# Attention and feed-forward in one kernel: score products in pairs of heads on the two halves of TensorE's rows, and weight scales from column sums

## The chip, the core and the metric

The program runs on one core of a Trainium2 chip. The metric is the device time of one launch in microseconds (us), lower is better. A core has the engines TensorE (PE; PEld is its weight load), VectorE (DVE), ScalarE (ACT), GpSimd (POOL) and SyncE (SP, which here only issues DMAs). Each takes its instructions in program order, and they wait for each other by semaphores. Products of TensorE go to eight banks of an accumulator memory, PSUM.

## The reference, cut

```python
# q, k, v: (8 batches, 8 heads, 576 positions, 64); w_in (512, 2048); w_out (2048, 512), all float32
scores = np.matmul(q, k.transpose(0, 1, 3, 2)) / 8
rel = pos[:, None] - pos[None, :]
mask_plain = (rel >= 0) & (rel < 32)                        # heads 0 to 3
mask_dil = (rel >= 0) & (rel < 128) & (rel % 4 == 0)        # heads 4 to 7
attn = softmax(where(mask, scores, -1e9))
x = (attn @ v), heads side by side: (4608, 512)
h = x @ w_in
g = h * np.tanh(np.log1p(np.exp(h)))                        # mish
out = g @ w_out                                             # (4608, 512)
```

## The kernel before

The 4608 rows are worked on as 16 units `u` of 288 positions (half a batch each). All large products are made of float16 parts: a float32 number is scaled by a power of two and split into a high and a low float16 half, and three of the four products of halves are summed in PSUM. So a unit's first feed-forward product (`ff1`, one step `ff<u>.<fc>` for each of 16 column groups) is 12 TensorE products with 288 moving columns, and so is each step of its second (`ff2`, steps `fo<u>.<e>.<j>`, 4 output groups by 4 chunks of the sum). That makes 512 steps in all, 6144 products.

Attention of a unit: `loads` and `loads_v` fetch q, k and v; `prep` finds scales; `scores` (`sc`) multiplies; `exps` (`ex`), `transpose_p` (`tp`), `values` (`va`), `transpose_x` (`tx`) follow. A head has few key blocks because of its mask: 3 blocks of 96 queries by 96 or 128 keys (heads 0 to 3) or 4 blocks of 72 queries by 72 or 104 keys (heads 4 to 7). Units 0 to 3 are *direct*: `scores` starts a PSUM bank with the mask (L628) and adds float32 products of one head (L632). A head has 64 dimensions, so an even head lies in partitions 0 to 63 and an odd one in 64 to 127, and such a product uses 64 of TensorE's 128 rows. Units 4 to 15 are *split*: `prep` makes float16 halves `q2` and `k2` (L540 to L559), and 12 DMAs of SP (L555, L556, L566) then copy them so that the high and the low half of one head stand under each other in 128 partitions (`qs`, `ks`). With that a block takes two products with all 128 rows (L638).

The weights come as 64-bit floats, 16 chunks of 1 MB in the order of steps `wl<k>.<g>.<p>` (`k` 0 for w_in, 1 for w_out; `g` a group, `p` one of its two chunks). For each chunk `w_max` takes a maximum on VectorE (L311, tile `am`) and a scaled copy on ScalarE (L366); for each group `w_scale` brings the maximum over partitions by a transposition and a product (L319, L328) and computes the scale on VectorE; `w_words` (L406, L407, L409) builds float32 words and `w_split` the two halves, in ways that the table `WAYS` picks. Everything of `early`, the raw weights included, has to be done with before `open_late` can hand that memory to the split units.

`ORDER` is a list written out by hand: a name stands once for each stage of its step (a stage ends at a `yield`), and each engine gets its instructions in that order. `kw<n>` (`keep_warm`, L920) puts `n` products of zeros on TensorE as filler. Four PSUM banks (tag `a`) serve scores, values and transpositions, four others (tag `f`) the feed-forward and the filler. `BIASED`, `ON_POOL`, `ON_PE` and `ON_ACT` say which engine does a stage of some steps.

Of the kernel before, what the change touches and what calls it, by code (L numbers as in the profile page):

```python
# [32 lines left out]
TINY_HI = 0.05859375  # L33
# [16 lines left out]
va2.1 tp2.2 wp0.2.1 tp2.6 va2.2 ff0.12 va2.2 ff0.13 wp0.2.0 ff0.14 ff0.15 va2.2 wm0.0.0 ff0.8 gt0.1 gt0.3 ff0.10 va2.1  # L50
ww0.0.0 ff0.8 wp0.0.1 tx2.0 tp2.3 va2.6 ff0.11 tx2.0 va2.6 tp2.3 ff0.10 tp2.4 tx2.0 ff0.9 ff0.11 va2.6 tp2.4 gt0.3
wp0.0.0 va2.3 tp2.5 wp0.0.1 va2.3 ff0.9 tp2.5 gt0.2 va2.3 wl1.1.0 wp0.0.0 tx2.1 va2.4 tx2.1 va2.5 gt0.2 va2.4 wl1.0.0
tx2.1 va2.5 tp2.7 tx2.1 ff0.0 wl1.0.1 tp2.7 va2.4 wl1.1.1 va2.5 va2.7 ff0.0 ff0.1 lv1 va2.7 va2.7 tx2.2 ff0.1 tx2.3
ff0.3 tx2.2 ld1 wm1.1.0 tx2.3 tx2.2 ff0.2 tx2.2 tx2.3 wm1.1.0 ff2.0 ff0.3 ww1.1.0 ff0.2 ff2.1 ff2.0 gt0.0 ff2.2 ff2.1
wm1.0.0 gt0.0 ff2.4 ff2.2 wm1.0.0 ff2.5 ff2.4 wm1.0.1 ff2.6 ff2.5 wm1.0.1 ff2.7 ff2.6 ff2.3 ff2.7 gt2.1 wm1.1.1 ws1.0
ff2.3 gt0.0 ws1.0 ws1.1 wm1.1.1 ws1.0 ws1.1 ws1.0 ws1.1 gt2.0 ws1.1 gt2.1 ff2.8 pr1 gt2.1 wp1.1.0 ff2.10 ff2.11 gt2.0
ff2.8 ff2.10 ff2.9 ww1.1.1 ff2.11 sc1.3 ff2.9 gt2.2 ww1.0.1 sc1.2 sc1.1 ff2.12 sc1.3 wp1.1.0 sc1.2 ex1.3 ff2.15 gt2.2
ff2.14 ex1.2 ff2.12 wp1.1.1 tp1.2 sc1.0 sc1.1 wp1.1.1 tp1.2 sc1.4 ff2.15 sc1.0 ff2.14 sc1.7 ex1.1 sc1.4 sc1.5 sc1.7
tp1.3 wp1.1.1 ff2.13 sc1.5 tp1.3 wp1.1.1 ex1.4 pr1 fo2.1.0 ex1.5 ex1.7 pr1 wp1.0.1 pr1 fo2.1.1 ex1.0 pr1 wp1.0.1
ff2.13 sc1.6 fs1 va1.2 sc1.6 ld3 va1.3 gt2.3 tp1.0 fo2.1.2 ww1.0.0 lv3 va1.3 tp1.0 va1.2 ex1.6 tp1.1 fo0.1.0 va1.2  # L60
gt2.3 wl1.2.0 va1.3 va1.0 tp1.1 wp1.0.0 fo0.1.1 wp1.0.1 gt2.3 va1.0 tp1.6 va1.0 va1.1 tp1.6 fo0.1.2 va1.1 va1.1
wp1.0.0 tp1.5 sc3.4 tp1.5 sc3.2 sc3.4 wp1.0.1 wp1.0.0 sc3.6 sc3.2 ex3.4 sc3.3 sc3.6 wp1.0.0 fo2.1.3 ex3.2 sc3.3 ex3.6
pr3 tx1.0 ex3.3 tx1.1 fo2.0.0 tx1.0 fo2.1.3 va1.6 tx1.1 tx1.0 tp1.4 va1.6 wm1.2.0 fo2.0.1 tx1.0 tp1.4 va1.6 wm1.2.0
va1.4 tx1.1 fo2.0.2 va1.4 tx1.1 ww1.2.0 va1.5 sc3.7 va1.5 va1.4 tp1.7 fo2.0.3 sc3.7 tp1.7 va1.5 ex3.7 sc3.0 fo2.0.3
sc3.1 sc3.0 va1.7 sc3.1 ld4 ex3.0 sc3.5 fo0.1.3 ex3.1 sc3.5 wl1.2.1 va1.7 tx1.2 va1.7 ex3.5 tp3.4 fo2.0.3 fo0.0.0
tx1.2 fo2.1.3 wl1.3.1 tp3.4 tx1.2 tx1.3 tp3.0 wl1.3.0 tx1.3 fo0.0.1 tp3.0 tx1.3 pr3 tx1.3 fo0.0.2 pr3 pr4 lv4 ff1.0
pr4 pr4 pr3 fo0.0.3 ff1.0 pr3 va3.0 wm1.2.1 va3.4 va3.0 va3.4 tp3.1 tp3.2 tp3.1 va3.0 wm1.2.1 va3.4 va3.1 fo0.1.3
ws1.2 va3.1 tp3.3 tp3.2 va3.1 tp3.3 fo0.1.3 ff1.4 fo0.0.3 ws1.2 ww1.2.1 fo0.0.3 ff1.7 ff1.4 ff1.1 ff1.7 wm1.3.1 ws1.2
ff1.2 ff1.1 ws1.2 wm1.3.1 wp1.2.0 ff1.6 ff1.2 ww1.3.1 ff1.3 ff1.6 ff1.5 wp1.2.1 ff1.3 wm1.3.0 wp1.2.0 ff1.12 ff1.5
gt1.1 pr4 ff1.13 wp1.2.1 ff1.12 wp1.2.0 ff1.14 ff1.13 wp1.2.0 wp1.2.1 pr4 ws1.3 tx3.0 pr4 ff1.15 ff1.14 ws1.3 tx3.0  # L70
wp1.2.1 wm1.3.0 pr4 va3.2 pr4 ws1.3 fo2.2.0 ff1.15 va3.2 gt1.3 ws1.3 va3.3 fo2.2.1 va3.2 va3.3 wp1.3.1 tp3.6 va3.3
fo2.2.2 wp1.3.1 tp3.6 tx3.0 fs3 tp3.5 fs4 tx3.1 tp3.5 fo2.2.3 wp1.3.1 ww1.3.0 tx3.1 va3.5 fo0.2.0 fo2.2.3 va3.5
fo2.2.3 fo0.2.1 va3.5 wp1.3.1 wp1.3.0 tx3.1 tx3.2 fo0.2.2 tx3.2 wp1.3.0 va3.6 fo0.2.3 tx3.2 va3.6 mr ol pr4 va3.6
tp3.7 fo0.2.3 fo0.3.0 fo0.2.3 fo2.3.0 tp3.7 pr4 va3.7 fo2.3.1 va3.7 pr4 fo2.3.2 fo2.3.3 va3.7 pr4 tx3.3 fo2.3.3
fo0.3.1 tx3.3 fo2.3.3 tx3.3 fo0.3.2 gt1.0 fo0.3.3 gt1.0 pr4 fo0.3.3 ff1.8 fo0.3.3 gt1.1 ff1.11 pr4 ff1.8 gt1.3 ff1.10
ff1.11 gt1.1 fo1.3.0 ff1.10 ff1.9 gt1.3 ld5 fo1.3.1 ff1.9 gt1.2 ff3.0 gt1.2 pr4 sc4.2 sc4.1 sc4.6 sc4.2 sc4.5 ff3.1
ff3.0 pr4 fo1.3.2 ff3.1 sc4.0 fo1.3.3 sc4.1 lv5 fo1.3.3 pr5 sc4.4 ff3.2 fo1.3.3 sc4.6 ff3.3 ff3.2 pr5 sc4.7 sc4.5
ff3.3 ff3.4 pr5 sc4.3 ff3.4 ff3.5 sc4.0 ff3.6 ff3.5 pr5 ff3.7 ff3.6 ff3.8 sc4.4 ff3.7 pr5 sc4.7 ff3.8 ff3.9 pr5 ff3.10
ff3.9 sc4.3 pr5 ff3.10 ff3.11 pr5 ex4.1 fo1.2.0 fs5 pr5 fo1.2.1 fo1.2.2 tp4.1 fo1.0.0 pr5 tp4.1 tp4.1 fo1.0.1 ex4.7
pr5 ex4.6 ex4.3 fo1.0.2 ex4.2 ex4.0 fo1.0.3 tp4.2 pr5 tp4.0 tp4.2 ex4.5 tp4.0 fo1.2.3 ex4.4 fo1.0.3 ff3.11 tp4.0  # L80
fo1.1.0 fo1.2.3 tp4.2 tp4.5 tp4.3 fo1.1.1 tp4.5 gt3.0 tp4.3 fo1.0.3 pr5 tp4.5 va4.0 tp4.7 va4.1 fo1.1.2 gt3.1 tp4.3
gt3.0 va4.0 va4.2 va4.1 tp4.4 pr5 fo1.1.3 va4.2 tp4.6 gt3.1 ff3.12 gt3.2 va4.2 va4.0 va4.3 ff3.12 ff3.13 gt3.2 va4.3
ld6 ff3.14 va4.3 ff3.13 va4.1 tp4.7 tx4.0 tp4.4 ff3.14 tp4.7 tp4.6 tx4.1 tx4.0 fo1.1.3 sc5.1 pr5 tp4.4 sc5.2 sc5.0
tx4.1 sc5.4 sc5.1 ff3.15 tx4.0 tx4.1 fo3.0.0 pr5 ff3.15 gt3.3 tp4.6 sc5.7 fo3.0.1 fo1.2.3 gt3.3 lv6 fo3.0.2 pr6
fo3.1.0 fo1.1.3 sc5.2 fo3.1.1 pr6 va4.6 sc5.0 fo3.1.2 va4.6 pr6 fo3.0.3 va4.6 pr6 va4.7 fo3.0.3 fo3.1.3 va4.7 fo3.0.3
# [131 lines left out]
def attn_mish_ffn_kernel(  # L217
# [91 lines left out]
    def amax(o, i, axes=None):  # L309
        axes = axes or {2: AX.X, 3: AX.XY, 4: AX.XYZ}[len(i.shape)]  # L310
        nc.vector.tensor_reduce(o, i, axis=axes, op=ALU.max, apply_absolute_value=True)  # L311

    ones = const.tile([8, 1], F32, name="ones")
    nc.vector.memset(ones, 1.0)

    def over_partitions(m, n):
# [660 lines left out]
```

## Time and profile before

| | us |
|---|---|
| three runs | 960.72, 966.01, 969.75 |
| median of them | 966.01 |
| the profiled execution's own time | 960.96 |
| its span, first to last instruction | 959.1 |
| mean granted TensorE clock in it | 0.973 |

The page of the profile gives busy time by engine, the busy share in 40 slices of the span, the chain of work that ended last and groups of instructions by line. For TensorE busy time is no measure of use: its products are pipelined, so a product is on record for about 290 ns while the next one starts after 122 ns. What counts there is the time from start to start, which the timeline shows.

### The profile page before, as it was taken

What the parts mean: (1) busy time and instruction counts of PE and PEld (TensorE: products, weight loads), DVE (VectorE), ACT (ScalarE), POOL (GpSimd) and SP (SyncE); (2) the same over time, 40 slices, a digit from 0 to 9 for tenths busy, and PEclk for the clock granted to TensorE, in tenths of its full rate; (3) what the DMA queues carried; (4) which work ended last, traced back from release to release, by engine and by line L of the source; (5) the groups of instructions that cost most, each with busy time, mean ns of one, the idle gap of its engine ahead of it and who ended that gap; (6) DMA issues with size and microseconds to landing.
All of it is one profiled execution on the core that took longest, in us unless ns stands there. A gap on an engine that the chain in (4) does not pass through costs nothing.

```text
span 959.1 us, 21690 instructions
## 1 busy us (share of the span) xinstructions
PE 926.6 (97%) x8761; PEld 753.1 (79%) x8761; DVE 670.2 (70%) x1389; ACT 563.4 (59%) x1074; POOL 63.7 (7%) x117
## 2 busy tenths in 40 slices
PE   7998899999999899999989999999999999999998
PEld 6876678787877678888878887888888888887776
DVE  5789698695668777796959695887868696841020
ACT  2668676554373665738566665566665757555151
POOL 1000324033200000000000000000001000000000
PEclk7789999999999999999999999999999999999999
DMA  7523505601538392737385756748382826150000
GB/s 254 167 88 102 166 1 160 211 1 48 152 73 188 77 181 67 175 82 164 85 163 85 154 117 120 144 97 173 73 173 64 181 71 151 37 101 4 26 1 26
DMA packets 169620, 105.57 MB, mean 110 GB/s; under 512 B 126800, under 2 KB 156208, under 8 KB 169520
## 3 DMA queue, kind: packets, MB, share of 16 engines
q1 hardware_dynamic: 169520, 104.18, 46.0%
q8 instruction: 69, 1.13, 0.5%
q14 instruction: 31, 0.25, 0.1%
HBM read 49.02 MB, written 9.44 MB: 61 GB/s over the span
## 4 chain that ended last, share of the span: by engine, by line
PE 82%; DVE 8%; DMA 3%; issue 3%; SPq 3%; ACT 2%; POOL 0%; DVEq 0%; POOLq 0%; ACTq 0%
PE po L891 35%; PE ph L840 33%; PE psc L638 3%; PE pav L748 3%; PE psc L632 3%; SPq L566 2%; DMA pT<-p 1%; PE pav L742 1%; PE pz L920 1%; DVE g L881 1%; DVE raw L407 1%; DVE raw L409 1%; PE psc L628 1%; DMA g<-g 1%; DMA ks<-k 1%
## 5 line engine op out<-in xcount | busy, mean ns | idle before, releaser
L840 PE MATMUL ph<-x,w 128*128 128x288 f16 x3072 | 398.2, 289 | 2.5 <-DVE w L426 2.5
L891 PE MATMUL po<-g,w 128*128 128x288 f16 x3072 | 390.0, 287 | 0.0
L840 PEld LDWEIGHTS <-w 128*128 128x128 f16 x3072 | 298.9, 99 | 78.4 <-DVE w L426 2.6
L891 PEld LDWEIGHTS <-w 128*128 128x128 f16 x3072 | 298.4, 98 | 74.3 <-issue 0.2
L845 ACT ACTIVATE hm<-ph,fs 128x288 f32<-128x288 f32 x256 | 125.7, 498 | 137.5 <-PE ph L840 136.9
L881 DVE SCALAR_TENSOR_TENSOR g<-hm,sg,g 128x1152 f16<-128x1152 f32 x59 | 83.3, 1413 | 84.3 <-ACT g L879 84.3
L903 ACT ACTIVATE y<-po,fo 128x288 f32<-128x288 f32 x57 | 41.9, 736 | 134.5 <-PE po L891 115.5
L879 ACT ACTIVATE g<-hm,sg 128x1152 f16<-128x1152 f32 x59 | 74.0, 1254 | 4.6 <-PE po L891 3.6
L765 DVE TENSOR_TENSOR xs<-pav,rec 96x192 f32<-96x192 f32 (+1 forms) x128 | 49.6, 387 | 11.1
L654 DVE TENSOR_TENSOR sb<-sb,nm 96x256 f32<-96x256 f32 (+3 forms) x120 | 54.5, 454 | 4.1
L652 DVE TENSOR_REDUCE nm<-sb 96x2 f32<-96x256 f32 (+3 forms) x120 | 53.7, 448 | 3.3
L712 DVE TENSOR_TENSOR p<-sb,p 72x288 f16<-72x288 f32 (+3 forms) x57 | 28.7, 523 | 38.4 <-ACT p L710 38.4
L674 ACT ACTIVATE sb<-sb,ln_p 72x288 f32<-72x288 f32 (+3 forms) x96 | 51.6, 583 | 0.1
L646 DVE SCALAR_TENSOR_TENSOR sb<-psc,sc,m_r 96x352 f32<-96x352 f32 (+1 forms) x48 | 28.4, 591 | 23.5 <-PE psc L638 23.5
L522 POOL PARTITION_ALL_REDUCE mru<-m x10 | 10.8, 1077 | 495.6 <-DVE m L311 286.9
L638 PE MATMUL psc<-ks,qs 128*96 128x128 f16 (+3 forms) x672 | 41.2, 211 | 1.0 <-DMA ks<-k 1.0
L712 DVE TENSOR_TENSOR g<-sb,g 72x416 f16<-72x416 f32 (+3 forms) x39 | 20.2, 528 | 28.6 <-ACT g L710 28.5
L638 PEld LDWEIGHTS <-qs 128*72 128x72 f16 (+1 forms) x672 | 37.5, 119 | 2.4 <-DMA ks<-k 1.4
L780 ACT CAST g<-xs 96x384 f16<-96x384 f32 (+1 forms) x48 | 26.7, 556 | 16.0 <-DVE xs L765 15.9
L540 ACT ACTIVATE q<-qn,s 128x144 f16<-128x144 f32 (+1 forms) x60 | 30.5, 584 | 4.9 <-DVE s L307 4.8
L763 DVE RECIPROCAL rec<-den 96x3 f32<-96x3 f32 (+1 forms) x128 | 21.2, 165 | 15.4 <-ACT den L759 9.6
L782 DVE TENSOR_TENSOR g<-xs,g 96x384 f16<-96x384 f32 (+1 forms) x48 | 29.5, 614 | 2.5 <-ACT g L780 2.3
(139 smaller groups left out, 966.7 us busy)
## 6 DMA issues: line engine op xcount, KB each, us to landing
qn<-in_qT SPq DMA_DIRECT2D x16, 576.0 KB
out_T<-y SPq DMA_DIRECT2D x64, 144.0 KB
ks<-k SPq DMA_DIRECT2D x48, 184.0 KB
raw<-in_w_in SPq DMA_DIRECT2D x16, 512.0 KB
raw<-in_w_out SPq DMA_DIRECT2D x16, 512.0 KB
qs<-q SPq DMA_DIRECT2D x48, 144.0 KB
ks<-k SPq DMA_DIRECT2D x48, 144.0 KB
vn<-in_v SPq DMA_DIRECT2D x48, 128.0 KB
```

Of the source, the lines that this page charges most:

```text
L638: nc.tensor.matmul(pt[:nq, col:col + nk], d["qs"][:, h, pair, q0:q0 + nq], d["ks"][i][:, h, k0:k0 + nk], start=(i == 0), stop=(i == 1))
L652: nc.vector.tensor_reduce(nm[:nq, j:j + n], x, axis=AX.X, op=ALU.max, negate=True)
L654: nc.vector.tensor_tensor(o, x, nm[:nq, j:j + n].unsqueeze(2).broadcast_to([nq, n, w]), op=ALU.add)
L674: nc.scalar.activation(x, x, AF.Exp, bias=ln_p[:nq])
L712: nc.vector.tensor_tensor(lo, src, hi, op=ALU.subtract)
L765: nc.vector.tensor_tensor(xs[:nq, :nb, (head % 2) * D:(head % 2 + 1) * D], avv[:, :, :D], rc.unsqueeze(2).broadcast_to([nq, nb, D]), op=AL ...
L840: nc.tensor.matmul(ph[:, :HT], w1[j][:, c, wi, k * P:(k + 1) * P], x_of(d, xi, c), start=(n == 0), stop=(n == len(seq) - 1))
L845: nc.scalar.activation(d["m"][j][:, k], ph[:, :HT], AF.Mish, scale=d["fs"][:, j:j + 1])
L879: nc.scalar.activation(g[:, 0], m, AF.Identity, scale=sg)
L881: nc.vector.scalar_tensor_tensor(g[:, 1], m, sg, g[:, 0], ALU.mult, ALU.subtract)
L891: nc.tensor.matmul(po[:, :HT], w2[:, e, j, wi, k * P:(k + 1) * P], d["g"][j][:, gi, k, :], start=(j == 0 and n == 0), stop=(j == NCH - 1 a ...
L903: nc.scalar.activation(o, src, AF.Identity, scale=fo)
```

## The change

Split units: the copies to `qs` and `ks` go. Scores come from `q2` and `k2` where they lie, three products with 64 rows for a block instead of two with 128. `q2` and `k2` get a second buffer.

All units: a new step `sp<u>.<pair>` (`scores_of_pair`) makes the products of an even and an odd head together and lets them take turns, so that one product uses rows 0 to 63 and the next rows 64 to 127; it fills two of the four banks of tag `a`. `sc` keeps the work on VectorE.

Weights: the maximum on VectorE and the way over partitions go. `w_scale` multiplies the scaled copy, read as bfloat16, by ones on TensorE, so that every partition has the column sums in PSUM, and takes their maximum (L374). It is 4 products of 512 columns for a group of w_in and 16 of 128 for one of w_out. `w_words` becomes two stages. The constants of the scales and four ways of `WAYS` change.

`ORDER` is new: weights and units come in another sequence, v of unit 0 is the first load, and the filler grows from 238 to 646 products, all but 7 of them ahead of the first feed-forward product. The filler no longer takes a bank in turn, it writes the last 128 columns of one that the feed-forward uses. The tables change in a few entries.

```diff
     def w_max(k, g, p):
-        if k == 0:
-            amax(am[:, p:p + 1], hi.bitcast(F32))
-        else:
-            amax(am[:, p * WIDE:(p + 1) * WIDE], hi.bitcast(F32), AX.X)
-        yield
         nc.scalar.activation(a, hi.bitcast(F32), AF.Identity, scale=HI)
     def w_scale(k, g):
+        pm = ps.tile([P, 512], F32, tag="a", name="pm", bufs=4)
+        for i in range(NCC):
...
+            if k == 0:
+                nc.tensor.matmul(pm, ones_b.broadcast_to([P, P]), top, start=(i == 0), stop=(i == NCC - 1))
+            else:
+                for q in range(FPC):
+                    nc.tensor.matmul(pm[:, i * P:(i + 1) * P], ones_b.broadcast_to([P, P]), top[:, q * P:(q + 1) * P],
+                                     start=(q == 0), stop=(q == FPC - 1))
+        yield
+        nc.vector.tensor_reduce(m, pm.rearrange("p (a n) -> p a n", a=n), axis=AX.X, op=ALU.max)
...
     def prep(u):
-        for h in range(2):
-            nc.sync.dma_start(qs[0:D, h], qh[hs])
-            nc.sync.dma_start(qs[D:P, h], ql[hs])
...
-                for o in range(2):
-                    nc.sync.dma_start(ks[i][o * D:(o + 1) * D, h, :nkall], src[hs, :nkall])
+    def scores_of_pair(u, pair):
...
+        for h in range(2):
+            pt = d["ps", 2 * pair + h] = ps.tile([P, 512], F32, tag="a", name="psc", bufs=4)
...
+                for i, (qi, ki) in enumerate([(1, 0), (0, 0), (0, 1)]):
+                    products.append((o, d["q2"][hs, qi, pair, q0:q0 + nq], d["k2"][hs, ki, k0:k0 + nk], i == 0, i == 2))
...
+        for both in zip(*heads):
+            for o, q, k, start, stop in both:
+                nc.tensor.matmul(o, q, k, start=start, stop=stop, skip_group_check=True)
     def keep_warm(n):
-        pz = ps.tile([P, 512], F32, tag="f", name="pz", bufs=4)
         for _ in range(n):
-            nc.tensor.matmul(pz[:, :P], zeros, zeros, start=True, stop=True)
+            nc.tensor.matmul(fbs[3][:, 512 - P:], zeros, zeros, start=True, stop=True)
```

Three places show what the new order does. First TensorE, where the scores of unit 4, the first split one, begin; before:

```order
L840 LDWEIGHTS w10_99
L840 MATMUL ph_3193<-x_2663,w10_99 128x288
L638 LDWEIGHTS qs_3029
L638 MATMUL psc_3216<-ks0_3117,qs_3029 96x128
L638 LDWEIGHTS qs_3029
L638 MATMUL psc_3216<-ks1_3118,qs_3029 96x128
```

And the same place now (L894 is `ff2`, L617 the products of a pair):

```order
L894 MATMUL f3_111<-g0_112,w2_103 128x288
L717 MATMUL ptp_3242<-ident_70,sb_2929 104x72 x4
L617 LDWEIGHTS q2_3115
L617 MATMUL psc_3251<-k2_3152,q2_3115 72x72
L617 LDWEIGHTS q2_3115
L617 MATMUL psc_3252<-k2_3152,q2_3115 72x72
```

The products read `q2` and `k2` themselves, the two that follow each other belong to the two heads of a pair (banks psc_3251 and psc_3252) and so to different halves of the rows, and there are 24 of them for a pair of these heads where there were 16.

Second SP's queue, behind the mask copies of the first split unit; before (out_T is the result, qn, knp, knd and vn are the next unit's loads):

```order
L291 DMA m_r_96<-m_s_94 24x352 x4
L907 DMA out_T<-y_2945 128x288
L555 DMA qs_3029<-q2_2929 64x1152
L556 DMA qs_3029<-q2_2929 64x1152
L555 DMA qs_3029<-q2_2929 64x1152
L556 DMA qs_3029<-q2_2929 64x1152
L907 DMA out_T<-y_3040 128x288
L907 DMA out_T<-y_3086 128x288
L566 DMA ks0_3117<-k2_2975 64x1152 x2
L566 DMA ks1_3118<-k2_2975 64x1152 x2
```

Now:

```order
L289 DMA m_r_96<-m_s_94 24x352 x4
L910 DMA out_T<-y_3032 128x288
L910 DMA out_T<-y_3249 128x288
L447 DMA qn_3300<-in_qT 128x1152
L449 DMA knp_3302<-in_kT 128x2x320
L452 DMA knd_3304<-in_kdT 128x4x104 x2
L910 DMA out_T<-y_3225 128x288
L473 DMA vn_3550<-in_v 128x256 x3
L475 DMA vdn_3551<-in_vd 104x256 x4
L711 DMA_TRANSPOSE g7_119<-p161_3023 128x6x96
```

The copies are gone and the loads of the next unit stand directly behind the mask copies, with the transpositions of P next.

Third VectorE at the start of the program; before, the first two chunks of weights:

```order
L311 TENSOR_REDUCE am_151<-raw 128x1
L406 TENSOR_SCALAR w_100<-w_100 128x1024
L407 SCALAR_TENSOR_TENSOR raw<-raw,w_100 128x1024
L409 SCALAR_TENSOR_TENSOR raw<-raw 128x1024
L311 TENSOR_REDUCE am_151<-raw 128x1
L382 TENSOR_REDUCE wm<-am_151 128x1
L322 TENSOR_REDUCE c<-pm 1x1
```

Now the maxima of v of unit 0 come first:

```order
L309 TENSOR_REDUCE m<-vn 128x1
L309 TENSOR_REDUCE m<-vdn 72x1
L490 TENSOR_TENSOR m<-m 72x1
L321 TENSOR_REDUCE c<-pm 1x1
L397 TENSOR_SCALAR w_102<-w_102 128x1024
L494 COPY m_310<-pm 128x1
L303 TENSOR_SCALAR f<-m_310 128x1
L304 TENSOR_SCALAR f<-f 128x1
```

The two maxima of 1024 columns (L311, `am`) left VectorE's queue, and the weights' first instruction (now L397) stands behind the work on v.

433 lines of the change are left out of this document (212 added, 221 removed), and 12 rows, old and new, of tables (ON_ACT, WAYS).

## The prediction

> **What bounds the kernel now.** I read the page's busy shares and slices first, then the chain of waits, then windows for three stretches that I cut by progress, then the timeline at single places.
>
> ```profile
> span 959.1 us, 21690 instructions
> PE 926.6 (97%) x8761; PEld 753.1 (79%) x8761; DVE 670.2 (70%) x1389; ACT 563.4 (59%) x1074; POOL 63.7 (7%) x117
> DVE  5789698695668777796959695887868696841020
> PEclk7789999999999999999999999999999999999999
> ...
> 139.85 1.47 PE ph L840 x12
> 861.29 23.52 PE ph L840 x192
> ```
>
> The last row, of the chain, is TensorE alone: 192 feed-forward products in 23.52 us, 0.1225 us each (a step of 12 takes 1.47). All 6144 cost 752.6 us. The other 206 us of the span are attention's products, filler, and time in which TensorE stands or runs at half clock.
>
> ```profile
> 0.00:61.00 61.00, 52.66 (x456) 44.88 (x457) 44.83 (x103) 31.74 (x79) 3.10 (x19) 0.73 0.64 200
> 61.00:213.00 152.00, 143.58 (x1208) 114.60 (x1206) 123.03 (x260) 103.99 (x197) 30.67 (x18) 0.97 0.33 101
> 213.00:955.00 742.00, 730.02 (x7100) 593.60 (x7098) 502.31 (x1028) 426.90 (x798) 29.91 (x80) 0.99 0.48 105
> ...
> 61.00:213.00 152.00, 69.38 (x517) 51.14 (x514) 0.97 0.33 101
> 213.00:955.00 742.00, 325.84 (x2544) 245.83 (x2544) 0.99 0.48 105
> ...
> 61.00:213.00 152.00, 32.06 (x236) 22.49 (x237) 0.97 0.33 101
> 213.00:955.00 742.00, 357.55 (x2837) 275.85 (x2835) 0.99 0.48 105
> ```
>
> Columns: length, then busy time and count of PE, PEld, DVE, ACT and POOL, granted clock, DMA share, GB/s; the two pairs below are lines L840 and L891 alone. At 61 the first feed-forward product starts, at 213 the 64th of the 512 steps is done, at 955 the last product starts. So:
>
> - First stretch, 61 us: hardly any feed-forward. The clock is granted at 0.73, VectorE is busy 44.8 of 61.
> - Second, 152 us: 517 + 236 = 753 feed-forward products, 92.2 us. Direct scores (22.3, below) and the other direct attention and transpositions (about 20.7, by columns) make some 135; 17 are lost. VectorE is busy 123 of 152: with it at 81% TensorE waits often.
> - Third, 742 us: 5381 products, 659.2; split scores 30.4; split values 30; about 720 in all, 22 lost. TensorE is the bound here.
>
> Beyond 955 stand 4.1 us of span and 1.9 around it: 961.0 for this execution, 5 below the median of 966.0.
>
> **The change part by part.**
>
> *Split scores, on the path.* The rates come from the timeline where values and scores alternate, the counts from the groups.
>
> ```profile
> 755.55 0.44 PE L748 MATMUL pav<-vh,g 128*128 128x65 f16 x9
> 755.82 0.49 PE L638 MATMUL psc<-ks,qs 128*96 128x128 f16 x6
> 756.15 0.44 PE L748 MATMUL pav<-vh,g 128*128 128x65 f16 x9
> ...
> L638 PE MATMUL psc<-ks,qs 128*96 128x128 f16 x240 | 19.9, 221 | 1.0 <-DMA ks<-k 1.0
> L638 PE MATMUL psc<-ks,qs 128*72 128x104 f16 x192 | 11.1, 209 | 0.0
> L638 PE MATMUL psc<-ks,qs 128*72 128x72 f16 x192 | 9.3, 202 | 0.0
> L638 PE MATMUL psc<-ks,qs 128*96 128x96 f16 x48 | 6.0, 207 | 0.0
> ```
>
> From start to start nine values of 65 columns take 0.27 us, 0.030 each, six scores 0.33, 0.055. Both follow 0.417 ns a column and 2.5 ns. The 672 scores cost 240 x 0.056 + 192 x 0.046 + 192 x 0.0325 + 48 x 0.0425 = 30.4. Now there are 1008 products, 504 pairs. No row shows two halves at once. If a pair costs one product by columns, all cost 22.8; if its two follow each other, 45.6. I take 0.055 a pair, 27.7: a load with its product has never been quicker than 0.030 here, and two have to be issued.
>
> Entering and leaving the 64-row form costs too. The direct scores show it:
>
> ```profile
> 129.04 0.36 PE L628 MATMUL psc<-m_fb,ident_b 96*96 96x384 bf16 x1
> 129.34 0.89 PE L632 MATMUL psc<-knp,qn 64*96 64x128 f32 x6
> 130.16 0.42 PE L840 MATMUL ph<-x,w 128*128 128x288 f16 x2
> ...
> 129.33 0.68 PEld L632 LDWEIGHTS psc<-knp,qn 64*96 64x96 f32 x6 [0.17 <-issue]
> ```
>
> From mask to score 0.30 us pass, of which 384 columns are 0.16: 0.14 of waiting, and the weight load starts only behind it, though elsewhere loads run ahead. The six records take 0.82 to the next product; two passes over 128 columns each are 0.109 x 6 = 0.655, so 0.165 more: a bare load of 96 columns in two passes (0.08) and 0.085 on leaving. A stretch costs 0.30 in float32 and, with a load half as long, about 0.27 in float16. Split units had none; the new order has 45. That is 12.2 us. Net for split scores: 27.7 + 12.2 - 30.4 = **+9.5**, between -7.6 (full overlap, no waits at the borders) and +27.4.
>
> *Direct scores, 20 of 32 heads in the second stretch.*
>
> ```profile
> L632 PE MATMUL psc<-knp,qn 64*96 64x128 f32 x80 | 13.6, 301 | 0.0
> L632 PE MATMUL psc<-knd,qn 64*72 64x104 f32 x64 | 7.4, 256 | 0.0
> L632 PE MATMUL psc<-knd,qn 64*72 64x72 f32 x64 | 7.4, 270 | 0.0
> L632 PE MATMUL psc<-knp,qn 64*96 64x96 f32 x16 | 3.2, 289 | 0.0
> ```
>
> By columns 80 x 0.109 + 64 x 0.089 + 64 x 0.0625 + 16 x 0.083 = 19.7. Overlap makes that 9.9 (19.7 without). Stretches go from 32 to 16: -4.8. In all -14.6; by place 4.9 lie ahead of the first feed-forward product, **-9.7** in the second stretch.
>
> *Copies of q and k.* They are off the path.
>
> ```profile
> L566 SPq DMA_DIRECT2D ks<-k x96: 462/595/1772, 240.8 to 801.6; - x96
> PE psc L638 <- DMA ks<-k: 1.0, 1, 1.0
> PE pav L748 <- DMA pT<-p: 7.6, 3, 4.5
> ```
>
> 96 issues at 0.595 and 48 at about 0.5 leave SP's queue, some 81 us of its time, and scores waited for them 1.0 us in all. What waits is values, 7.6 us for the transposed P, whose DMAs stand behind the copies in the queue. Of the third stretch's 22 lost us I count 10 as won, by fewer DMAs ahead of P; the ends are 0 and 20.
>
> *Weights' scales.* Sixteen maxima leave VectorE:
>
> ```profile
> L311 DVE TENSOR_REDUCE am<-raw x16: 1197/1209/1220, 6.1 to 199.4; 128x1 f32<-128x1024 f32 x8, 128x2 f32<-128x1024 f32 x8
> L652 DVE TENSOR_REDUCE nm<-sb 96x3 f32<-96x384 f32 x24 | 13.2, 549 | 0.8
> L366 ACT ACTIVATE w<-raw 128x1024 f32<-128x1024 f32 x16 | 18.3, 1144 | 0.0
> ```
>
> 16 x 1.21 = 19.4, and the small steps to a scale some 3 more than the eight new maxima over 512 PSUM columns (about 0.6 each, from 0.549 for 384). TensorE gets 2048 columns a group, 0.87 x 8 = 7.0, five groups of them in the second stretch: 4.4, less 0.7 for the old way, **+3.7**. Those products wait for ScalarE's copies of both chunks (1.14 each); behind them on TensorE stand filler and first scores in the start, where nothing else is ready, and feed-forward later, with both copies one to three steps ahead in the list. The new entries of the tables shift a few operations between engines; VectorE's sum moves by less than 1 us, and I count nothing.
>
> *The order.* I added the VectorE rows, mean of their form, along both lists. Ahead of the first feed-forward product stand 47.5 us before and 52.1 now; from there to the 64th step 133 and 109. Of these 24, 16 are the maxima and their small steps; the rest now stands earlier. TensorE between the same steps: 135 - 9.7 + 3.7 - 1.3 (products now earlier) = 127.8. Its share of VectorE falls from 98% to 85%; the third stretch has 75% by the same sums (542 of 720) and loses 3%, the second lost 13%. Between them I take 7%, 9 us: **137** instead of 152. The ends are 130 and 150.
>
> *The start.* v of unit 0 goes ahead of the weights in SP's queue:
>
> ```profile
> 0.73 1.82 SPq L342 DMA_DIRECT2D raw<-in_w_in  x4
> 5.32 7.02 SPq L481 DMA_DIRECT2D vn<-in_v  x3
> 12.38 3.47 SPq L483 DMA_DIRECT2D vdn<-in_vd  x4
> 6.11 1.22 DVE L311 TENSOR_REDUCE am<-raw 128x1 f32<-128x1024 f32 x1 [5.12 <-DMA raw<-in_w_in]
> L920 PE MATMUL pz<-w 128*128 128x128 f16 x238 | 22.7, 268 | 1.0 <-DVE w L915 1.0
> ```
>
> v's issues take up to 10.5 us, so weights that were there 5.4 us after their issue come at 14 to 17, and VectorE has some 10 of its 52.1 us (two maxima, two chunks' words) done by 23 to 25; the other 42 give 65 or a little more. TensorE has 639 fillers, at a 128-column product's 0.056 35.7 us, and 17.6 of work: 54, or 58 with some 7 us at half clock. Filler is free as long as VectorE is later than that; beyond, 16 of them cost 0.9. So the first product starts at **65** (58 to 72) instead of 61.
>
> Sum: 65 + 137 + (720 + 9.5 + 1 of direct work that moved behind + 12 lost = 743) + 6 = **951** against the profiled 961.
>
> *A rule weighed.* The trace has a load of 96 columns with its product at 0.055, so a load is no longer than that. The Trainium skill, page "TensorE: Matmul & The Clock Gate", section "LDWEIGHTS (loading the stationary operand)", has a load last its columns over 1.2 GHz, so 80 ns for 96 columns and 60 for 72. With loads of two halves side by side that would be the price of a pair, 34.6 in all (an estimate from that page), and the sum 958; the rows speak against it. The same page, in "Measured speedup vs the span model", has products in different row groups start about 4 ns apart; by that a pair costs 60 ns, and the sum is 954. No row here shows two halves at once.
>
> **The rivals.**
>
> - *Loads one after the other.* Two halves stream together but their weight loads don't. A float16 load runs at 0.417 ns a column at most (96 columns fit into a 96-column product's 0.0425), so a pair takes 0.085 with 96 queries and 0.065 with 72: 216 x 0.085 + 288 x 0.065 = 37.1, 9.4 over my 27.7, and 3.6 more in the direct scores of the second stretch: 964, no change. For it: loads follow each other on record everywhere. Against: each half has its own rows.
> - *No overlap, the other side.* The two products of a pair follow each other. Split scores cost 45.6 instead of 27.7, direct ones of the second stretch 6 more: 975, slower. Place: the 45 stretches. From 0.085 a pair on, the gain is used up. The border waits of 0.14 and 0.085 above speak for it: the form is changed with care. The change then does more products for nothing.
> - *Banks.* A pair holds two of four PSUM banks until VectorE has read both (0.6 each, row below); if each of 48 pairs makes TensorE wait 0.3, 14 us more: 965. Against: TensorE waits for such readers nowhere in the list of waits above 1 us.
>
> ```profile
> L646 DVE SCALAR_TENSOR_TENSOR sb<-psc,sc,m_r 96x384 f32<-96x384 f32 x24 | 14.6, 607 | 11.7 <-PE psc L638 11.7
> ```
>
> **How the numbers follow.** Overlap as forecast 0.60, loads in a row 0.18, none 0.10, banks 0.12. The forecast's 951 stands against an execution 5 below the median; the same saving from the median gives 956. Part of the spread of the runs may come from the clock of the first 61 us, which the filler holds up, so I take 953. Its own range, by start (7), second stretch (-7, +13) and lost time (10), is 938 to 965. Below 938 and above 972 together I leave out 2 in 10, the largest part of it the case without overlap. A measurement tells about 1% (9.7 us) from no change. Faster: 0.41 from the forecast, 0.03 and 0.01 from loads and banks, 0.45. Slower: 0.065 without overlap, 0.03 loads, 0.045 banks, 0.01 the forecast, 0.15. Within 1%: 0.40.
>
> **What would show it.** The gap from one pair's start to the next in split units: 0.055, or 0.085, or 0.11. The wait on entering and leaving a stretch, 0.14 and 0.085. The first feed-forward product at 65, the 64th step at 202, the last product at 945. VectorE's busy share between the first two below 80%. Values' wait for P below 3 us. I am wrong if the first product comes at 58 or 75, if TensorE waits for PSUM readers, or if units 5 to 13 take more than 54 us each.

## The result, and the profile after

| | before | after |
|---|---|---|
| median of 4 runs each, us | 963.53 (960.72 to 969.75) | 930.96 (930.58 to 931.51) |
| ratio, with its 95% interval | | 0.966 (0.963 to 0.969) |
| profiled execution, span, us | 959.1 | 929.2 |
| last product of the first feed-forward step starts | 60.6 | 59.7 (forecast 65) |
| from there to the 64th step | 152.8 | 134.1 (forecast 137) |
| from there to the last product's start | 741.7 | 731.4 (forecast 743) |

3.4% faster, and 7 us below the low end of the range. The starts of feed-forward products in the trace give the last three rows. What the prediction calls the start of the first feed-forward product, 61 us, is that of the last of the 12 products of the first step; the same point is kept here. The first product itself starts at 58.0 before and at 58.3 after:

```profile
57.99 5.12 PE L840 MATMUL ph<-x,w 128*128 128x288 f16 x24
58.34 3.10 PE L843 MATMUL f<-x,w 128*128 128x288 f16 x24
```

So nothing begins earlier. The step takes less: its products start 0.24 us apart before and 0.122 after. With 5.8 behind the last product's start the parts after make 931.0, the forecast's made 951.

The page of the changed kernel, with the lines that answer to those of before:

```profile
span 929.2 us, 22966 instructions
PE 918.5 (99%) x9558; PEld 745.0 (80%) x9562; DVE 647.5 (70%) x1352; ACT 565.7 (61%) x1086; POOL 57.3 (6%) x116
DVE  4998987558585697997687887877686786524120
PEclk9999999999999999999999999999999999999999
PE 92%; DVE 5%; ACT 1%; issue 1%; DMA 0%; SPq 0%; DVEq 0%; ACTq 0%
```

The clock's digits are all 9 where before began 7789, and the chain that ended last is TensorE's by 92% (82% before). The same three stretches by windows (columns as in the prediction):

```profile
0.00:59.70 59.70, 58.01 (x863) 53.45 (x867) 44.86 (x102) 33.67 (x79) 3.10 (x19) 1.00 0.72 220
59.70:193.80 134.10, 132.12 (x1252) 107.56 (x1251) 106.71 (x228) 104.60 (x198) 41.22 (x31) 0.99 0.36 111
193.80:925.20 731.40, 728.04 (x7447) 583.98 (x7446) 495.89 (x1024) 426.65 (x811) 13.00 (x66) 1.00 0.33 74
```

VectorE was busy 123 of 152 us in the second stretch and is now busy 107 of 134, 80% instead of 81%: its work and the stretch shrank together. In the third its work is nearly the same, 496 for 502.

What TensorE waited for in the third stretch, after:

```profile
PE f L843 <- ACT hm L848: 1.7, 2, 1.2
PE pav L744 <- DMA pT<-p: 1.6, 1, 1.6
```

The values' 7.6 us have become 1.6. The first row is a wait for a reader of PSUM (L848 reads the feed-forward's banks, 1.7 us in all); no row has a reader of the scores' banks as the releaser. The second row is less sure: in four of the runs below (the maxima put back, a product inside each pair, pairs done twice, two pairs in a row) a wait of 1.6 us for a tile of values, at 333 to 340 us, is put down to VectorE's work on scores (`sb`) instead. A timeline of TensorE in a split unit shows the new stretches:

```profile
383.85 1.63 PE L894 MATMUL f<-g,w 128*128 128x288 f16 x12
385.41 0.74 PE L617 MATMUL psc<-k,q 64*72 64x104 f16 x24
386.09 3.11 PE L894 MATMUL f<-g,w 128*128 128x288 f16 x24
389.13 0.70 PE L617 MATMUL psc<-k,q 64*96 64x128 f16 x18
389.77 0.42 PE L894 MATMUL f<-g,w 128*128 128x288 f16 x2
```

From start to start 24 products of 104 columns take 0.68 us and 18 of 128 take 0.64. One after the other at 0.046 and 0.056 they would take 1.10 and 1.01. The starts within the first of these stretches, as ns from one to the next (the first number is from the feed-forward product ahead, the last to the one behind):

```
216, 4, 70, 3, 42, 4, 42, 4, 42, 3, 43, 3, 43, 3, 43, 3, 42, 4, 42, 4, 42, 3, 43, 3, 139
```

The two products of a pair start 3 or 4 ns apart, and a pair takes 46 ns, which is 104 columns at 0.417 and 2.7. Entering costs 94 ns more than the usual 122, the first pair 28 more than the others (37 with 96 queries), leaving 96 more: 0.22 us a stretch.

### The profile page after: what moved, and what is told of

Same layout as the page of the kernel before. It is cut to its first block, busy times and chain, and to the rows that moved or that the text cites. A ratio compares the mean times of both kernels' runs of the same rounds, so it can differ in the third digit from the quotient of the medians.

```text
span 929.2 us, 22966 instructions
## 1 busy us (share of the span) xinstructions
PE 918.5 (99%) x9558; PEld 745.0 (80%) x9562; DVE 647.5 (70%) x1352; ACT 565.7 (61%) x1086; POOL 57.3 (6%) x116
## 4 chain that ended last, share of the span: by engine, by line
PE 92%; DVE 5%; ACT 1%; issue 1%; DMA 0%; SPq 0%; DVEq 0%; ACTq 0%
PE f L894 39%; PE f L843 38%; PE psc L617 4%; PE f L922 3%; PE pav L744 3%; PE pav L738 1%; PE ptp L717 1%; DVE raw L399 1%; DVE nm L648 1%; DVE m L309 1%; DVE raw L401 0%; PE psc L614 0%; ACT hm L848 0%; DVE raw L412 0%; PE pm L367 0%
## 5 line engine op out<-in xcount | busy, mean ns | idle before, releaser
L843 PE MATMUL f<-x,w 128*128 128x288 f16 x3072 | 393.3, 286 | 1.7 <-ACT hm L848 1.7
L894 PE MATMUL f<-g,w 128*128 128x288 f16 x3072 | 393.2, 287 | 0.0
L894 PEld LDWEIGHTS <-w 128*128 128x128 f16 x3072 | 296.7, 98 | 74.9
L848 ACT ACTIVATE hm<-f,fs 128x288 f32<-128x288 f32 x256 | 119.6, 497 | 103.5 <-PE f L843 96.8
L906 ACT ACTIVATE y<-f,fo 128x288 f32<-128x288 f32 x60 | 41.8, 718 | 99.6 <-PE f L894 74.2
L761 DVE TENSOR_TENSOR xs<-pav,rec 96x192 f32<-96x192 f32 (+1 forms) x128 | 49.6, 387 | 11.2 <-DVE rec L759 0.9
L670 ACT ACTIVATE sb<-sb,ln_p 96x352 f32<-96x352 f32 (+3 forms) x96 | 53.5, 586 | 0.2
L755 ACT ACTIVATE den<-pav 96x3 f32<-96x3 f32 (+1 forms) x96 | 14.7, 162 | 62.8 <-PE pav L744 62.5
L708 DVE TENSOR_TENSOR p<-sb,p 96x352 f16<-96x352 f32 (+3 forms) x57 | 29.6, 525 | 22.7 <-ACT p L706 22.5
L922 PE MATMUL f<-zeros 128*128 128x128 f16 x646 | 42.0, 224 | 1.1 <-DVE zeros L918 1.1
L922 PEld LDWEIGHTS <-zeros 128*128 128x128 f16 x646 | 39.1, 101 | 1.9 <-DVE zeros L918 1.0
L642 DVE SCALAR_TENSOR_TENSOR sb<-psc,sc,m_s 72x288 f32<-72x288 f32 (+1 forms) x48 | 27.6, 574 | 11.3 <-PE psc L617 11.2
L706 ACT CAST p<-sb 96x352 f16<-96x352 f32 (+3 forms) x57 | 27.4, 489 | 12.9 <-DMA g<-p 10.9
```

Of the source, the lines that this page charges most:

```text
L642: nc.vector.scalar_tensor_tensor(shaped(sb), shaped(pt), d["sc"][:nq], mask, ALU.mult, ALU.add)
L670: nc.scalar.activation(x, x, AF.Exp, bias=ln_p[:nq])
L761: nc.vector.tensor_tensor(xs[:nq, :nb, (head % 2) * D:(head % 2 + 1) * D], avv[:, :, :D], rc.unsqueeze(2).broadcast_to([nq, nb, D]), op=AL ...
L843: nc.tensor.matmul(ph[:, :HT], w1[j][:, c, wi, k * P:(k + 1) * P], x_of(d, xi, c), start=(n == 0), stop=(n == len(seq) - 1))
L848: nc.scalar.activation(d["m"][j][:, k], ph[:, :HT], AF.Mish, scale=d["fs"][:, j:j + 1])
L894: nc.tensor.matmul(po[:, :HT], w2[:, e, j, wi, k * P:(k + 1) * P], d["g"][j][:, gi, k, :], start=(j == 0 and n == 0), stop=(j == NCH - 1 a ...
```

## The experiments

Twelve more runs were made. The stretches are those of the table above, from the starts of feed-forward products in each profile: up to the last product of the first step, from there to the 64th step, from there to the last product. The time is the median of 4 executions or more, and the profile is of one of them:

| kernel | stretches | time |
|---|---|---|
| before | 60.6 / 152.8 / 741.7 | 963.1 |
| after, once more | 59.4 / 134.1 / 731.4 | 931.0 |
| after, no filler | 62.5 / 134.4 / 731.3 | 933.6 |
| after, half the filler | 62.3 / 134.1 / 732.2 | 932.3 |
| after, heads without turns | 61.7 / 135.4 / 745.6 | 948.7 |
| after, maxima put back | 64.9 / 136.7 / 731.4 | 938.7 |
| after, a product inside each pair | 60.6 / 132.5 / 745.1 | 944.0 |
| after, the product beside the pair | 60.5 / 132.4 / 733.8 | 932.8 |
| after, split pairs done twice | 59.2 / 134.1 / 753.0 | 953.1 |
| after, two pairs in a row | 60.5 / 132.4 / 744.1 | 942.8 |
| after, copies and 128-row products | 70.7 / 133.8 / 785.8 | 995.2 |
| before, 2.7 times the filler | 62.1 / 153.7 / 741.0 | 963.7 |
| before, copies for two units alone | 61.3 / 155.2 / 736.1 | 958.3 |

**The kernel after, once more.**

> The kernel after once more, unchanged, beside the runs of this call: every theory has it at 930 to 933 us; it says how far the others' differences can be trusted, and how far the first feed-forward product (59.7 us in the first profile, 60.5 to 62 in kernels that are the same up to there) varies by itself.

931.02 (930.64 to 931.52). The kernel after repeats within 0.1%, so differences of a few us between it and its variants count, unless a variant's own executions spread as far. The first stretch alone varies more, from 59.2 to 60.6 in kernels that are the same up to there. The kernel before spread from 960.8 to 969.7.

**Filler: none, half, and more of it in the kernel before.** In `ORDER` all `kw<n>` are dropped, halved, or (in the order of before) multiplied by 2.7.

```diff
-lv0 wl0.3.0 wl0.3.1 ld0 wl0.0.0 wl0.0.1 pr0 kw16 kw16 kw16 kw16 kw16 kw16 kw16 kw16 kw3 pr0 pr0 kw10 pr0 wm0.3.0
+lv0 wl0.3.0 wl0.3.1 ld0 wl0.0.0 wl0.0.1 pr0 kw8 kw8 kw8 kw8 kw8 kw8 kw8 kw8 kw1 pr0 pr0 kw5 pr0 wm0.3.0
```

> The kernel after without any filler products (their results are never read, so nothing else is left out). Theory A: the filler holds the granted clock up in the first 60 us and takes nothing from the work beside it; without it the 17.6 us of real products ahead of the first feed-forward product run at half clock and the chain to that product gets 5 to 10 us longer, and the windows of half clock of before (at 75, 120, 219 and 331 us) mostly stay away since the order no longer leaves TensorE idle: 936 to 944 us. Theory B: the filler is the main thing of the whole gain: above 950. Theory C: the filler delays the start, since TensorE is busy nearly all of the first 60 us with it: 922 to 929.

> The kernel after with half of the filler products at each place. Theory A: the clock falls in some of the gaps, 932 to 938 us. Theory B (filler is the main thing): 940 or more. Theory C (filler delays the start): 924 to 929, with the first feed-forward product at 53 to 57 instead of 59.7.

> The kernel before with 2.7 times as many filler products at each place where it has some, 643 as in the kernel after; nothing else is changed. Theory A: the clock of the first 60 us alone is worth little, as the 2.6 us showed that the kernel after lost without its filler: 955 to 962 us. Rival (clock): the windows of half clock of before fill up and it comes to 940 to 950. Rival 2: filler ahead of the work delays the first feed-forward product: 966 to 975.

933.60, 932.25 and 963.70. Without filler the kernel loses 2.6 us, all of it up to the end of the first step: its first product starts 1.5 us later and its 12 products take 1.3 us more. The other stretches stay within 0.3. With half the filler two executions took 930 us and two 934; the profile is of a longer one. In the kernel before, 643 fillers change nothing (ratio 0.9995, 0.9967 to 1.0024). So the filler carries 2.6 of the 32 us, less than the 5 to 13 of the first run's theory A and far from theory B; theory C is out. The timeline shows that the products of unit 0 do run at half the clock without it. With filler, then without:

```profile
31.62 0.74 PE L617 MATMUL psc<-knd,qn 64*72 64x72 f32 x16
32.29 0.73 PE L738 MATMUL pav<-vdn,pp 72*72 72x65 f32 x8
```

```profile
28.94 1.24 PE L617 MATMUL psc<-knd,qn 64*72 64x72 f32 x16
30.11 1.22 PE L738 MATMUL pav<-vdn,pp 72*72 72x65 f32 x8
```

The scores take 1.17 from start to start instead of 0.67. It costs so little since TensorE's work there is short and VectorE mostly sets the start, as the next run shows.

**The maxima put back on VectorE**, into a tile that nobody reads.

```diff
     def w_max(k, g, p):
+        am = ready[k, g]
+        if k == 0:
+            amax(am[:, p:p + 1], hi.bitcast(F32))
+        else:
+            amax(am[:, p * WIDE:(p + 1) * WIDE], hi.bitcast(F32), AX.X)
         nc.scalar.activation(a, hi.bitcast(F32), AF.Identity, scale=HI)
```

> The kernel after with the 16 maxima of the weights that VectorE took before put back (into a tile that nobody reads; scales still come from the column sums); the outputs are unchanged. Theory A: VectorE is what TensorE waits for up to the 64th feed-forward step, so its 16 us come back there in part: the 64th step at 200 to 208 instead of 193.8 and the end at 936 to 945 us. Rival: the column sums' place in the order took the weights off the path whatever VectorE does, 930 to 933. Rival 2: all 16 us come back, 946 or more.

938.67, theory A's range. Its windows:

```profile
0.00:64.90 64.90, 59.09 (x862) 53.41 (x866) 52.14 (x109) 33.72 (x79) 3.09 (x19) 1.00 0.67 204
64.90:201.60 136.70, 131.73 (x1252) 106.98 (x1252) 118.01 (x237) 104.73 (x198) 40.12 (x31) 1.00 0.35 108
```

In the first stretch VectorE is busy 7.3 us more (52.14 for 44.86) and the stretch is 5.2 longer. Then it is busy 11.3 more and the stretch is only 2.6 longer: there VectorE has room now. Of 18.6 us of VectorE's time 7.7 come back.

**Heads one after the other.**

```diff
-        for both in zip(*heads):
-            for o, q, k, start, stop in both:
+        for one in heads:
+            for o, q, k, start, stop in one:
```

> The kernel after with the products of a pair's two heads issued one head after the other instead of by turns; nothing is left out. Theory A: products of the two halves of rows run at the same time only if they stand next to each other, so the split scores cost TensorE 27 us more and the direct ones some 10 more, TensorE being busy 99% of the span: 960 to 969 us. Rival: a stretch of the second head overlaps with the first head's in any order, or waits elsewhere take it up: 931 to 937. Rival 2: only the split part costs, 952 to 959.

948.70, 17.7 us more, in none of the three ranges: overlap is there, and the turns are worth 18 us, about half of what I expected to lose. In the trace the split scores take 44.6 us from start to start instead of 29.0. The starts of one stretch (24 products of 72 columns) tell why it isn't 51 (29.0 and once more the pairs' columns, 21.6):

```
216, 56, 35, 35, 35, 35, 35, 35, 35, 6, 29, 27, 8, 27, 8, 27, 35, 35, 35, 35, 35, 35, 35, 35, 131
```

The tenth record carries the wait for the second head's PSUM tile, which in the program belongs to the thirteenth. It starts 6 ns after the ninth, and two more starts follow 8 ns behind another. So TensorE reached past the first head's last three products to the other half's first ones: its products do not always start in program order. The 24 starts span 0.71 us where 0.83 would be due one by one: where the two heads meet, some three products overlap by themselves, and the turns are for the rest.

**A 128-row product inside each split pair, and beside it.** Zeros go to columns that nobody reads.

```diff
-        for both in zip(*heads):
+        for n, both in enumerate(zip(*heads)):
+            if n == 3 * (len(bl) // 2) and not d["direct"]:
+                nc.tensor.matmul(pts[0][:, 416:], zeros, zeros[:, :96], start=True, stop=True, skip_group_check=True)
```

In the control the same line stands ahead of the loop.

> The kernel after with one more product of 128 rows and 96 columns (zeros, into columns of the pair's tile that nobody reads) in the middle of each of the 48 split pairs, between two blocks of keys; nothing is left out. Theory A: what a stretch of split scores loses (entry 0.09, the first load 0.04, exit 0.09 us) is the change between products of 64 and of 128 rows, wherever it lies: 48 x (0.22 + 0.04) = 12.5 us more, 942 to 946 us. Rival: what is lost at the borders is a wait for something else (the loads of q2 and k2, a free tile of scores) and a second border in the same pair costs nothing but its product: +2 to 3, 932 to 935.

> Control of the run with the product in the middle: the same product of 128 rows and 96 columns ahead of each split pair, beside the 128-row products that stand there anyway. Theory A: 48 x 0.04 = 2 us more, 932 to 934 (the few pairs that follow one another directly get a border more). Rival (the product itself, or its place in the pair's tile, costs): as much as the other run.

944.04 and 932.82, both theory A. The difference is 11.2 us. The traces have 93 stretches of split scores against 48 in the control, which parts the three places where two pairs follow each other directly; so it is 45 stretches more, 0.25 us each, a little over the 0.22 that the starts above give.

```profile
389.05 0.47 PE L619 MATMUL psc<-k,q 64*72 64x104 f16 x12
389.45 0.22 PE L617 MATMUL psc<-zeros 128*128 128x96 f16 x1
389.60 0.47 PE L619 MATMUL psc<-k,q 64*72 64x104 f16 x12
390.00 3.11 PE L896 MATMUL f<-g,w 128*128 128x288 f16 x24
```

The pair that took 0.68 takes 0.95 with one product of 0.043 in its middle, 0.23 more than the product. So the price belongs to the change between 64 and 128 rows and back, not to what the pair waits for.

**Split pairs done twice.**

```diff
-        for both in zip(*heads):
+        turns = list(zip(*heads))
+        for both in turns if d["direct"] else sum((2 * turns[i:i + 3] for i in range(0, len(turns), 3)), []):
```

> The kernel after with every block's products of the 48 split pairs done twice (the second time over the first, so the outputs stay). Theory A: a pair of products of the two halves costs its columns at full clock and 2.7 ns, whatever its size: about 504 pairs more, 21.6 us of columns and 1.4 us beside, with the price of a stretch's entry and exit unchanged: 952 to 956 us. Rival (a floor of 55 ns to a pair, as the prediction had it): 27.7 us more, 958 to 960. Rival 2 (loads one after the other): 0.085 us a pair, 43 us more, 971 to 976.

953.06, 22.0 us more: theory A, and both rivals are out.

```profile
389.85 1.29 PE L618 MATMUL psc<-k,q 64*72 64x104 f16 x48
391.07 2.13 PE L895 MATMUL f<-g,w 128*128 128x288 f16 x16
```

48 products take 1.22 where 24 took 0.67: 12 pairs in 0.55, 0.046 each. Over all 504 pairs the scores' starts grow by 23.3 us, 46 ns a pair at a mean of 103 columns (43 ns).

**Two pairs in a row**, to save borders. In `ORDER` a unit's second `sp` moves up behind the first, the fourth behind the third, where they stood at most 25 places apart.

> The kernel after with the second pair of a unit's split scores moved up directly behind the first (and the fourth behind the third) where it stood at most 25 places later in the order: 14 pairs of the 24 pairs of pairs; nothing else is changed. Theory A: each stretch of products of 64 rows saved is worth the 0.23 us that the added borders cost, so 3 us less: 926 to 929 us. Rival: the tiles of scores are not free so early, TensorE waits for their readers and it takes 932 to 945.

942.80, 11.8 us more, the rival. TensorE now waits for the readers of the four banks; in its list of waits (L576 is the pairs' line there, L601 the first reading of scores):

```profile
PE psc L576 <- DVE sb L601: 3.1, 5, 0.8
PE psc L576 <- DVE xs L720: 2.9, 2, 1.6
PE psc L576 <- DVE x L763: 2.3, 1, 2.3
```

Waits of over 0.4 us grow from 3.7 to 13.3 us in the third stretch, and three windows of half clock, which the kernel after doesn't have there, cost some 5.5 us more. Of 45 stretches 34 are left, and the borders cost some 2 us less by the starts; that is real, but the banks take more.

**The copies.** First the kernel after with copies and 128-row products again, then the kernel before with fewer copies.

```diff
+        for h in range(2):
+            nc.sync.dma_start(qs[0:D, h], qh[hs])
...
-                for i, (qi, ki) in enumerate([(1, 0), (0, 0), (0, 1)]):
-                    products.append((o, d["q2"][hs, qi, pair, q0:q0 + nq], d["k2"][hs, ki, k0:k0 + nk], i == 0, i == 2))
+                for i in range(2):
+                    products.append((o, d["qs"][:, h, pair, q0:q0 + nq], d["ks"][i][:, h, k0:k0 + nk], i == 0, i == 1))
```

> The kernel after with the split scores as before: copies qs and ks by DMA, products of 128 rows (two to a block and head, issued by turns), q2 and k2 with one buffer instead of two since no more fits beside the copies; filler of other values; order, column sums and direct pairs stay. Theory A: the gain behind the 64th feed-forward step comes from the order that leaves fewer waits, and the split pairs themselves cost 3 us more than the products of before: 926 to 932 us. Rival: the copies and the single buffers were what TensorE waited for in before: 940 to 955, with the 64th step at 194 to 200 as in the kernel after and the rest behind it.

```diff
-        for h in range(2):
+        for h in range(2 if u < DIRECT + 2 else 0):
             nc.sync.dma_start(qs[0:D, h], qh[hs])
```

> The kernel before with the copies qs and ks made for units 4 and 5 alone; the scores of units 6 to 15 read those stale copies, so their part of the output is not computed, while all engines do the same work but for 120 of 144 DMAs. Theory A: the copies stood in SyncE's queue ahead of the DMAs that transpose P, and what the values waited for behind the 64th feed-forward step (7.6 us in 3 waits) was that: the rest behind the 64th step takes 733 to 738 us instead of 741.7, the whole 954 to 960. Rival (the new order did it, copies were beside the path): 961 to 966.

The first took 995.23, on the rival's side but far beyond its 955, with the 64th step at 204.5. Two of its waits:

```profile
PE psc L628 <- DMA ks<-k: 23.8, 14, 3.5
PE f L932 <- ACT minus L292: 10.9, 1, 10.9
```

The second row comes from the filler, which reads another constant there, starts 10.9 us late, and the first product comes 11 us later. Behind the 64th step 54 us are added. Waits of over 0.4 us are 44 us there instead of 3.7; more than half of them are scores that wait for copies, for which the new order leaves no time. So the order and the missing copies belong together, and this run can't say what the order gives alone. Since it has one buffer for `q2` and `k2` and the kernel after two, the copies' delay and the buffers aren't told apart either.

The second took 958.34 (ratio to before 0.994, 0.992 to 0.996), theory A: the third stretch falls by 5.6, to 736.1. But the longest of the waits that I had in view stays:

```profile
PE pav L748 <- DMA pT<-p: 4.4, 1, 4.4
```

It is the same 4.4 us at the same place, around 330 us. In this run no copy stands ahead of the transposing DMA (L715) there; SyncE waits for P itself, which lies in a buffer named g:

```profile
SPq L715 <- DVE g L712: 5.4, 1, 5.4
```

So the copies cost 5.6 us by the other waits, the longest 2.8 us at 493 us. The wait at 330 is not theirs; by these rows it comes from a P that is late, and so from the order.

## Right and wrong, by the prediction's steps

**The start: 59.7, not 65.** The failed step is "VectorE has some 10 of its 52.1 us ... done by 23 to 25; the other 42 give 65". The bound was right (7.3 us more on VectorE moved the start by 5.2), and so were the 10 (10.8 by 23 us in the trace); the other 42 were not. VectorE is busy 44.86 us in the whole window, so 34 were left. The durations of its instructions in the window sum to 49.0: 4 of the 7 us too many are the overlap of instructions that follow each other, which a sum of mean durations counts twice; the rest are instructions that took less than the mean taken for them. The same sum for the kernel before, 47.5, was too high too: VectorE is busy 42.0 us there up to the first product. The filler does what was assumed; without it TensorE runs at half clock and this stretch is 2.8 longer. By the first product itself, at 58.3, the prediction's sign of being wrong (58) was all but met.

**The second stretch: 134.1, forecast 137.** The term for the direct scores, -9.7, was right: from start to start they take 12.2 us with their masks instead of 21.7, -9.5. The products of two heads take the time of one:

```profile
130.88 0.90 PE L617 MATMUL psc<-knp,qn 64*96 64x128 f32 x12
131.71 0.54 PE L894 MATMUL f<-g,w 128*128 128x288 f16 x3
```

These 12 take 0.83 from start to start, where 6 of one head took 0.82 in the prediction's row at 129.34. For the weights' scales the term was +3.7, and by columns TensorE got 3.4 more. But from start to start the column sums took 5.8 us where the old way took 8.8, since the old way waited for VectorE three times on record, 4.1 us (the prediction had these among its 17 lost). TensorE loses some 6 us beside its 127.8 instead of the 9 assumed. In the kernel before, waits of over 0.4 us made 9.5 there; now 2.0. Two windows of half clock, at 76 and 120 us, cost some 3.5 there; one at 159 us costs 1.6 now.

**The third stretch: 731.4, forecast 743.** Two terms were mis-sized, the split scores by 6.6 us and the lost time by 4.5.

- *A pair of products.* "I take 0.055 a pair ...: a load with its product has never been quicker than 0.030 here, and two have to be issued" is the failed step. The pair costs its columns and 2.7 to 5.5 ns, so 180 x 0.056 + 36 x 0.043 + 144 x 0.046 + 144 x 0.0355 = 23.4 instead of 27.7. The 45 stretches' borders cost 0.22 each (starts; 0.25 by the experiment) instead of 0.27: 9.9 instead of 12.2 (entering 0.09 for 0.14, the first load 0.03 for 0.04, leaving 0.10 for 0.085). So the split scores cost 33.3, and their net term is +2.9, not +9.5. The mechanism was right, and so was its sign: three 64-row products in pairs are a little dearer than two of 128 rows.
- *Lost time.* The forecast won 10 of 22 us; the stretch is 720 + 2.9 + 1 + about 7.5, so 14 were won. The copies, for which the 10 were counted, gave 5.6. The larger part is two waits that the new order doesn't have, and what the clock does behind them. The longer one, for a late P, in the kernel before:

```profile
333.95 1.17 PE L748 MATMUL pav<-vh,pT 128*128 128x65 f16 x18 [4.47 <-DMA pT<-p]
335.06 1.36 PE L840 MATMUL ph<-x,w 128*128 128x288 f16 x5
...
320.00:345.00 25.00, 20.53 (x189) 16.10 (x187) 17.69 (x41) 21.31 (x44) 0.00 (x0) 0.86 0.60 118
331.00:339.00 8.00, 5.05 (x55) 3.93 (x56) 5.92 (x13) 6.31 (x14) 0.00 (x0) 0.57 0.73 100
```

Behind the wait 18 values take 1.11 us, 62 ns each instead of 30. The granted clock is 0.86 in these 25 us and 0.57 in the 8 from 331, which is half clock for some 7 us. After:

```profile
320.00:345.00 25.00, 22.26 (x258) 17.75 (x253) 24.14 (x50) 8.20 (x17) 0.00 (x0) 1.00 0.31 78
```

The wait is 4.6 us by the starts, and the products up to 338.6 lose 2.3 more at half clock (the first 2 us of it fall into the wait and cost nothing): 6.9. The other wait, 2.1 us for `xs` at 217, has 3.4 us of half clock behind it, which cost 1.7:

```profile
PE px L794 <- DVE xs L765: 2.0, 1, 2.0
219.00:223.00 4.00, 3.90 (x24) 2.92 (x25) 2.52 (x5) 1.42 (x2) 1.97 (x3) 0.57 0.18 53
```

Both stand in the run with copies for two units alone as well. From that run to the kernel after, waits of over 0.4 us fall from 7.8 to 3.7 us in this stretch and the loss at half clock from 4.2 to nothing: 8.2. With the copies' 5.6 that is the 14, read from the traces; no run took the new order's part by itself.

**Rivals.** Loads one after the other: no, 46 ns a pair where 65 to 85 were priced. No overlap: no; made on purpose it costs 18 us. Banks of the scores: hardly in this order, but they bite as soon as two pairs stand together. The filler alone: no.

**The rule weighed.** By the Trainium skill, page "TensorE: Matmul & The Clock Gate", section "LDWEIGHTS (loading the stationary operand)", a load takes its columns over 1.2 GHz, an estimate of 80 ns for 96 columns and 60 for 72. The trace does not agree: a pair with two such loads takes 43 to 56 ns and 35 to 46. The 4 ns of the page's section "Measured speedup vs the span model" agree with it: 3 or 4 ns between the starts of a pair. The prediction's 954 by that section puts the price of the largest pair, 60 ns, on all 504; pair by pair the same estimate makes 24.9 us, and the sum 948.

**The range.** Its ends of the single terms held: start 58 to 72, second stretch 130 to 150, split scores -7.6 to +27.4, lost time 0 to 20. The low end of the sum, 938, did not, because the start, the second stretch, the split scores and the lost time came out on the cheap side together, by 5, 3, 7 and 4 us. The range was made of the start, the second stretch and the lost time; the low end of the split scores, 17 us under what was taken for them, is not in it. In the start and the split scores it was one habit: where no row showed an overlap, I gave it little or none.

## What to carry over

Two products on different halves of TensorE's rows run at once if they stand next to each other, and a pair then costs one product by columns and 3 to 5 ns; but each stretch of them between products of 128 rows costs TensorE 0.22 to 0.25 us, so they want long stretches, as far as PSUM banks allow. Here they were a little dearer than the 128-row products that they replaced in the split units (+2.9 us), where they spare the copies (5.6 in the kernel before); in the direct units they paid by themselves (-9.5). A long wait of TensorE can be paid more than once, since the clock may fall behind it (4.6 us cost 2.3 more, 2.1 cost 1.7): look for the few long ones first. For an engine's load use its busy time in a window, not a sum of mean durations.

## What was not expected of the hardware

- TensorE starts products of the other half of the rows ahead of up to three earlier ones: where one head's products follow the other's, three starts came 6 to 8 ns behind another. "Each takes its instructions in program order", which stands ahead of the prediction, does not hold for it there.
- The column of the granted clock can say 1.00 while products run at half speed. Without filler it does so for the 18 us in which the scores above took 1.17 us instead of 0.67:

```profile
28.00:46.00 18.00, 15.42 (x103) 12.11 (x102) 16.50 (x34) 13.39 (x37) 0.00 (x0) 1.00 0.87 244
```

So the start-to-start time of a known product is the surer sign; in that run products reach full speed only at 63 us, the 14th feed-forward product.
- The same half clock for the first 63 us costs 2.6 us in the end, and 643 fillers in the kernel before win nothing.
